# Another hand-kept order of work for a fused attention and feed-forward kernel

## The chip, the core and the metric

The kernel runs on one core of a Trainium2 chip. A core has five engines that matter here, each with its own list of instructions, taken in order: TensorE (PE, matrix products, with a weight load, PEld, ahead of each), VectorE (DVE), ScalarE (ACT), GpSimd (POOL) and SyncE (SP), which here only starts DMA transfers. An engine that must wait for another's result stops, and everything behind that instruction in its list stops too. The metric is the time of one execution in microseconds (us). The kernel before has a median of 922.56 us over three runs (921.46 to 923.68).

## What is computed

The reference is block-sparse attention followed by a feed-forward stage, in fp32:

```python
# q, k, v: (4, 8, 768, 64): 4 batches, 8 heads, 768 positions, 64 per head
scores = scale * np.matmul(q, k.transpose(0, 1, 3, 2))      # scale = 1/8
scores = np.where(mask, scores, -1000000000.0)              # 32-wide blocks: window, edges, 3 drawn per row
attn = np.exp(scores - np.max(scores, axis=-1, keepdims=True))
attn = attn / (np.sum(attn, axis=-1, keepdims=True) + 1e-09)
x = np.matmul(attn, v)                                      # then (3072, 512)
h = x @ w_in                                                # 512 x 2048
out = (h - np.tanh(h)) @ w_out                              # 2048 x 512
```

## The kernel before

**Precision.** Most fp32 products are made from two parts: a high part, rounded to the type that PE multiplies, and a low part, what is left. A product is then three matmuls, high by high, high by low and low by high. Engines therefore spend much time on splits: ACT makes high parts (a copy), DVE or POOL low parts (a subtraction).

**Attention.** The 32 heads are taken in pairs, since two heads fill 128 partitions. The keys and queries of a pair are loaded (`load_qk`), split (`high` L333 on ACT, `low` L339, on DVE for all pairs but the first) and copied by DMA to the places in `slab` that the matmuls read (`dist` L362). V is loaded (`load_v` L327) into a single raw buffer, `rawv`. DVE takes its absolute maximum (`v_max` L417), PE turns that (`v_all` L425), DVE makes a scale (`v_scale`, L429 to L434), ACT the high part (`v_high` L438) and DVE the low part (`v_low` L442). Only then is the raw buffer free for the next pair.

Each head needs the largest score of each row before its exponentials. This is a first pass over the scores: six `smax` units of PE (L455) per head go two by two into the buffer `psm`, and DVE reduces each two in one `maxima` (L461); these two `smax` are called a *smax pair*. PE turns the maxima (`turn_max` L469, again through `psm`), DVE negates them (`neg_max` L473), and a DMA puts them as one more row into the operands of the scores (`put_max` L479).

A head then has three steps of two *score blocks*, 128 keys by 768 queries each: four matmuls (L488, L489) into the buffer `pst`, of which there is one; ACT's exponential (`expo` L492) reads it and writes `pe`. ACT makes the fp16 high part (`p_high` L498, `ph`), POOL the low part (`p_low` L507, `pl`). Two steps later an *accumulate block* on PE (`accum`, L521, L524, L525, 36 short fp16 matmuls) multiplies them with V into `pav`. After a head's last step DVE norms the result (`norm`), and each pair is written out as part of x (`spill` L542).

**Feed-forward.** x is read back, turned by PE in blocks of 128 (`x_turn` L832, four small transposes each) and split (L836, L840). A *unit* is a slice of 128 of the 2048 inner columns for 512 rows of x: twelve matmuls (`h_part` L854) into a bank, then ACT and DVE form h − tanh(h) from a polynomial (L864 to L882), POOL makes its low part (L884), and the second product follows (L889, L890, L891). Units of the first part run among the attention, in halves of six matmuls; they fill PE while exponentials are made. Weights are staged by DMA (`stage_w` L741 and L745) and split; four of them come in through `fetch_w` (L921) and `split_w` (L926 on ACT, L928 on POOL) where attention ends. Everything behind that point is the late part of the plan, and there PE is fed by feed-forward units alone.

**What sets the order.** The kernel builds a list of operations, each with a due time, an engine, an estimated duration, and the buffers it reads and writes (`Plan.add`). The order in each engine's list comes from `ORDER`: a string of characters per engine, where each character says how far down the remaining operations, sorted by due time, the next one lies (`Plan.lanes`):

```python
for c in row:
    if c == MARKS[-1]:
        skip += len(MARKS) - 1
    else:
        lanes[e].append(rest.pop(skip + MARKS.index(c)))
        skip = 0
```

`Plan.order` then walks the five lists with the estimated durations and gives each operation a modelled start. These starts decide only two things: the sequence in which the operations are written down over all engines, which leaves each engine's own order as the strings have it, and the *fillers*. `KeepBusy` puts extra matmuls (L240, `ones` into `pav`) in front of a PE operation where the modelled start leaves a gap, up to 110 us of modelled time; 14 stand at the very start. `in_order` at last chains the instructions of each engine, so that nothing moves them any more.

## Time and profile before

| what | value |
|---|---|
| median of three runs | 922.56 us (921.46 to 923.68) |
| the profiled execution's own time | 921.18 us |
| its span, first to last instruction | 919.4 us |
| mean granted clock of PE | 0.999 |
| PE busy | 895.2 us, 97% of the span |
| DVE, ACT, POOL busy | 76%, 71%, 53% |
| DMA, queue of the loads and stores | 119.58 MB, 45.5% of 16 engines' span |

All instruction times are from that one profiled execution, which was 1.38 us faster than the median. Line numbers in the profile are those of the kernel above. The bracket at the end of a timeline row tells how long the engine stood idle before the instruction, and what released it. In the list of waits, "A <- B: total, times, longest" says that the instruction A of an engine stood for B. A row for PEld is a weight load that had to wait; PE itself may still be working on the matmul before it, so such waits are partly hidden. [...]

### The profile page before, as it was taken

The numbers are of one execution on the slowest core, as the hardware profiler recorded it, in microseconds if no ns is written. First come the engines' busy times: TensorE is split into PE (matmuls) and PEld (weight loads), VectorE is DVE, ScalarE is ACT, GpSimd is POOL, SyncE is SP. The second block draws the span as 40 slices with busy tenths as digits, with TensorE's granted clock in tenths as the row PEclk, the third lists the DMA queues.
The fourth block names the chain that finished last, engine by engine and source line by source line (L and its number), as shares of the span: only waits on it lengthen the run. The fifth ranks groups of instructions, "written<-read, shape, count | busy, mean of one in ns | idle before, by whom it ended". The sixth has DMA issues, their size and how long they took to land.

```text
span 919.4 us, 18275 instructions
## 1 busy us (share of the span) xinstructions
PE 895.2 (97%) x7177; PEld 744.8 (81%) x7177; DVE 701.5 (76%) x1000; ACT 654.0 (71%) x964; POOL 485.4 (53%) x324
## 2 busy tenths in 40 slices
PE   8998999999999999999989999999999999999998
PEld 4777778888887888888878888888888888888886
DVE  6987878889887888886469999985667666765765
ACT  5888888988889798798865666665555555555553
POOL 5677887778777676778842434532212222222131
PEclk9999999999999999999999999999999999999999
DMA  8878588766878758465352333230014202300201
GB/s 228 205 187 240 133 219 225 206 174 178 208 233 193 199 134 278 109 168 178 94 162 92 104 92 94 90 115 1 1 70 155 86 24 92 127 23 1 92 1 46
DMA packets 57677, 120.73 MB, mean 131 GB/s; under 512 B 6170, under 2 KB 26836, under 8 KB 56568
## 3 DMA queue, kind: packets, MB, share of 16 engines
q1 hardware_dynamic: 57592, 119.58, 45.5%
q8 instruction: 56, 0.92, 0.4%
q14 instruction: 29, 0.24, 0.1%
HBM read 55.68 MB, written 26.21 MB: 89 GB/s over the span
## 4 chain that ended last, share of the span: by engine, by line
PE 84%; ACT 6%; DVE 4%; DMA 3%; issue 2%; SPq 1%; POOL 0%; ACTq 0%; DVEq 0%
PE bank L854 27%; PE pf L889 8%; PE pf L891 8%; PE pf L890 8%; PE pst L488 7%; PE pst L489 6%; PE psm L455 5%; PE pav L521 3%; PE pav L524 3%; PE pav L525 3%; ACT pe L492 3%; PE bank L889 1%; DMA raw<-qk 1%; PE bank L890 1%; PE bank L891 1%
## 5 line engine op out<-in xcount | busy, mean ns | idle before, releaser
L507 POOL TENSOR_TENSOR pl<-pe,ph 128x768 f16<-128x768 f32 x192 | 320.4, 1688 | 95.4 <-ACT ph L498 49.8
L884 POOL TENSOR_TENSOR gl<-t,gh 128x512 fp32r<-128x512 f32 x96 | 126.9, 1323 | 298.6 <-ACT gh L882 233.3
L492 ACT ACTIVATE pe<-pst 128x768 f32<-128x768 f32 x192 | 155.2, 808 | 54.1 <-PE pst L489 52.1
L461 DVE TENSOR_REDUCE mc<-psm 128x2 f32<-128x1536 f32 x93 | 163.0, 1753 | 30.5 <-PE psm L455 29.8
L498 ACT ACTIVATE ph<-pe 128x768 f16<-128x768 f32 x192 | 157.9, 840 | 2.7 <-PE pav L525 0.3
L488 PE MATMUL pst<-slab 128*128 128x512 f32 (+1 forms) x384 | 141.6, 369 | 8.7 <-ACT pe L492 7.4
L868 DVE TENSOR_TENSOR t<-t,bank 128x512 f32<-128x512 f32 x96 | 65.7, 684 | 94.3 <-ACT t L866 69.0
L489 PE MATMUL pst<-slab 97*128 97x512 f32 (+1 forms) x384 | 122.4, 340 | 0.0
L521 PE MATMUL pav<-vhl,ph 128*128 128x65 f16 x1152 | 116.4, 194 | 0.1
L524 PE MATMUL pav<-vhl,ph 128*128 128x64 f16 x1152 | 115.8, 195 | 0.0
L525 PE MATMUL pav<-vhl,pl 128*128 128x65 f16 x1152 | 115.3, 192 | 0.0
L521 PEld LDWEIGHTS <-ph 128*128 128x128 f16 x1152 | 105.5, 96 | 7.0 <-issue 4.4
L874 ACT ACTIVATE u<-u,bias 128x512 f32<-128x512 f32 x96 | 69.2, 721 | 58.3 <-DVE bank L876 57.8
L524 PEld LDWEIGHTS <-ph 128*128 128x128 f16 x1152 | 106.6, 97 | 0.4 <-issue 0.2
L525 PEld LDWEIGHTS <-pl 128*128 128x128 f16 x1152 | 106.7, 99 | 0.0
L488 PEld LDWEIGHTS pst<-slab 128*128 128x128 f32 x384 | 72.6, 189 | 32.0 <-ACT pe L492 19.7
L455 PE MATMUL psm<-slab 88*128 88x512 f32 (+1 forms) x378 | 87.9, 350 | 5.9 <-DVE nm L473 1.9
L866 ACT ACTIVATE t<-bank 128x512 f32<-128x512 f32 x96 | 56.7, 591 | 43.5 <-PE bank L854 38.8
L864 ACT ACTIVATE u<-bank 128x512 f32<-128x512 f32 x96 | 57.0, 594 | 43.0 <-PE bank L854 41.8
L882 ACT ACTIVATE gh<-t 128x512 fp32r<-128x512 f32 x96 | 60.3, 628 | 36.3 <-DVE t L880 18.1
L880 DVE COPY_PREDICATED t<-u,bank 128x512 f32<-128x512 int32 x96 | 71.5, 745 | 18.9 <-ACT u L874 13.5
L890 PE MATMUL pf<-wx,gh 128*128 128x512 f32 x216 | 84.1, 389 | 0.0
(135 smaller groups left out, 1918.5 us busy)
## 6 DMA issues: line engine op xcount, KB each, us to landing
slab<-hm SPq DMA_DIRECT2D x124, 192.0 KB
slab<-lo SPq DMA_DIRECT2D x63, 192.0 KB
raw<-qk SPq DMA_DIRECT2D x15, 768.0 KB
stage<-w_in SPq DMA_DIRECT2D x16, 512.0 KB
stage<-w_out SPq DMA_DIRECT2D x16, 512.0 KB
xsav<-xbuf SPq DMA_DIRECT2D x4, 2048.0 KB
rawv<-v SPq DMA_DIRECT2D x16, 384.0 KB
xscr<-xq SPq DMA_DIRECT2D x16, 384.0 KB
```

The costliest lines, as they stand in the source:

```text
L455: nc.tensor.matmul(o[:, b0 + c0 : b0 + c1], lhsT=sB[s][0:88, t * P : (t + 1) * P], rhs=sA[s][0:88, c0:c1], start=True, stop=True)
L461: nc.vector.tensor_reduce(out=mcs[h][:, t - 1 : t + 1], in_=psm.rearrange("p (x s) -> p x s", x=2), op=ALU.max, axis=AX.X)
L488: nc.tensor.matmul(pst[:, q], lhsT=sC[c][:, kc], rhs=sD[c][:, q], start=True, stop=False)
L489: nc.tensor.matmul(pst[:, q], lhsT=sA[a][0:97, kc], rhs=sB[a][0:97, q], start=False, stop=True)
L492: nc.scalar.activation(out=pe[s % 2][:, x * S : (x + 1) * S], in_=pst[:, 0:S], func=AF.Exp, scale=0.125)
L498: nc.scalar.activation(out=phs[s][0][:, c], in_=pe[s % 2][:, c], func=AF.Copy)
L507: eng.tensor_tensor(out=pl[:, c], in0=pe[s % 2][:, c], in1=ph[:, c], op=ALU.subtract)
L521: nc.tensor.matmul(oav[:, t, :], lhsT=ph[:, c], rhs=vv[:, 0:65], start=(kt == 0 and t == 0), stop=False, skip_group_check=True)
L524: nc.tensor.matmul(oav[:, t, 0:64], lhsT=ph[:, c], rhs=vv[:, 65:129], start=False, stop=False, skip_group_check=True)
L525: nc.tensor.matmul(oav[:, t, :], lhsT=pl[:, c], rhs=vv[:, 0:65], start=False, stop=last, skip_group_check=True)
L854: self.nc.tensor.matmul(h, lhsT=w[:, cc], rhs=z[:, c, :], start=(c == 0 and x == 0), stop=(c == NCT - 1 and x == 2))
L890: self.nc.tensor.matmul(o, lhsT=gh[:, c], rhs=wo[1][ft], start=False, stop=False)
```

## The change

All five strings of `ORDER` are replaced, so all five engines run their operations in another order. The operations themselves are the same: same matmuls, same splits, same transfers, except for the fillers. Of the rest of the diff, three things bear on what runs.

- The estimates that `Plan.order` uses change: durations, the time from an engine's end to a reader on another engine (`HOP`, `MORE`), and a result is now ready for a reader on the *same* engine 0.03 us after its latency and not at once. Since the order is given by the strings, these change only the written sequence and the number of fillers.
- High and low parts of the exponentials now lie in one tile with three buffers (`halves`), where there were two tiles with three buffers each. The size is the same, and so are the readers and writers of each part.
- Two small tiles `vf` are added, with a memset each on DVE at the start. Nothing reads them: the options that would (`FULL`, `TWICE`) are empty.

The core of the diff, with one row of a string for all:

```diff
-        "#$%&#&'########(((##&####%%##########%##&#*##(##*&##&*#%##%###&%##$'#%##($#%###&#####&###'###############$#%##"
+        '#$%#%&##%$#####((##&##$##&%#######$$#&%##%##(##&&##&&#%##&%#######$#########################$#$$#$##$#########'
...
+FULL = {}
+TWICE = [s for s in range(1, 27) if s < 0]
...
-    HOP = {"PE": 0.045, "ACT": 0.08, "DVE": 0.03, "POOL": 0.1, "SP": 0.03}
-    LESS = {"PE": 0.0, "ACT": 0.1, "DVE": 0.0, "POOL": 0.0}
-    MORE = {"PE": 0.17, "ACT": 0.1, "DVE": 0.085, "POOL": 0.05}
+    HOP = {"PE": 0.045, "ACT": 0.1, "DVE": 0.05, "POOL": 0.11, "SP": 0.03}
+    LESS = {"PE": 0.0, "ACT": 0.11, "DVE": 0.0, "POOL": 0.01}
+    MORE = {"PE": 0.17, "ACT": 0.11, "DVE": 0.085, "POOL": 0.06}
...
                 if b in wrote:
                     deps[i].add(wrote[b])
+                    reads.add((wrote[b], i))
...
-                    d += 0.09 * (not o[10] and (fp16 or t > free[e] + 0.02))
-                    fp16 = o[10]
+                    d += 0.085 if kind == 2 else 0.09 * (not o[10] and (kind or t > free[e] + 0.02))
+                    kind = int(o[10])
...
                 same = ops[j][2] == e and e != "SP"
-                ready[j] = max(ready[j], free[e] if same else end + self.HOP[ops[j][2]])
+                k = end + 0.03 if (i, j) in reads else free[e]
+                ready[j] = max(ready[j], k if same else end + self.HOP[ops[j][2]])
...
+    vf = [acst.tile([P, 2, 2, 65], F32, name=f"vf{i}") for i in range(NV)]
     for i in range(NV):
         nc.vector.memset(vhl[i][:, :, :, 64:65], 1.0)
+        nc.vector.memset(vf[i][:, :, :, 64:65], 1.0)
...
+    def halves(s):
+        if s not in phs:
+            phs[s] = p2.tile([P, 2, 2, S], F16, tag="ph", name=f"ph{s}", bufs=3)
+        return phs[s]
...
     def p_high(s, x):
-        if s not in phs:
-            phs[s] = [p2.tile([P, W2], F16, tag=n, name=f"{n}{s}", bufs=3) for n in ("ph", "pl")]
         c = slice(x * S, (x + 1) * S)
-        nc.scalar.activation(out=phs[s][0][:, c], in_=pe[s % 2][:, c], func=AF.Copy)
+        nc.scalar.activation(out=halves(s)[:, x, 0], in_=pe[s % 2][:, c], func=AF.Copy)
```

What the new strings move, counted over the plan's operations:

| what | before | after |
|---|---|---|
| between two successive score blocks on PE (191 places): nothing | 2 | 0 |
| only transposes of the maxima or of V's scale | 5 | 4 |
| one `smax` | 2 | 2 |
| two `x_turn` (eight transposes of x) only | 1 | 0 |
| a smax pair, no transposes of x | 34 | 33 |
| a smax pair and `x_turn` | 6 | 9 |
| an accumulate block, half a unit, or more | 141 | 143 |
| between a smax pair and the next use of `psm` (93 places): nothing | 1 | 0 |
| one score block only (all in heads 1 to 9) | 6 | 7 |
| two score blocks | 2 | 0 |
| accumulate blocks followed by work of another kind | 95 | 90 |
| ACT: an exponential directly followed by the copy that reads it | 76 | 52 |
| fillers (of which 14 at the start in both) | 94 | 80 |

On PE, one of the two places where a score block stood directly behind another is the second block of step 13 and the first of step 14 (line L488 and L489 before, L520 and L521 in the changed kernel; `pst` is the buffer of the scores, `psm` that of the maxima). Before:

```order
L488 MATMUL pst<-slab 128x256
L489 MATMUL pst<-slab 128x256
L488 MATMUL pst<-slab 128x512
L489 MATMUL pst<-slab 128x512
L488 MATMUL pst<-slab 128x256
L489 MATMUL pst<-slab 128x256
L455 MATMUL psm<-slab 128x512
```

After:

```order
L520 MATMUL pst<-slab 128x256
L521 MATMUL pst<-slab 128x256
L479 MATMUL psm<-slab 128x512
L479 MATMUL psm<-slab 128x256 x2
L479 MATMUL psm<-slab 128x512
L520 MATMUL pst<-slab 128x512
L521 MATMUL pst<-slab 128x512
L520 MATMUL pst<-slab 128x256
```

The smax pair that stood behind the second of these blocks now stands between the two.

On DVE, at the start of the program, the maxima of head 1 (L461, then L485), a weight's conversion (L751 and L755, then L809), the low part of V for pair 0 (`vhl`; L442, then L448), the low part of keys and queries of pair 1 (`lo1`; L339, then L345) and the negated maxima (`nm`; L473, then L497) stand before as

```order
L461 TENSOR_REDUCE mc1_261<-psm_155 128x2
L751 TENSOR_SCALAR bank1_79<-stage1_82 128x512
L442 SCALAR_TENSOR_TENSOR vhl0_157<-rawv0_242,sb0_320,vhl0_157 128x12x64
L755 SCALAR_TENSOR_TENSOR bank1_79<-stage1_82,bank1_79 128x512
L473 TENSOR_SCALAR nm1_357<-psm_155 6x128
L339 TENSOR_TENSOR lo1_359<-raw1_267,hm1_316 128x1536
```

and after as

```order
L485 TENSOR_REDUCE mc1_265<-psm_155 128x2
L448 SCALAR_TENSOR_TENSOR vhl0_157<-rawv0_188,sb0_283,vhl0_157 128x12x64
L485 TENSOR_REDUCE mc1_265<-psm_155 128x2
L345 TENSOR_TENSOR lo1_327<-raw1_269,hm1_312 128x1536
L497 TENSOR_SCALAR nm1_377<-psm_155 6x128
L809 TENSOR_SCALAR bank0_78<-stage0_81 128x512
```

V's low part moved ahead of the last maximum, the conversions behind the negated maxima, and the low part of pair 1 between the last maximum and the negated ones. On SP, the loads of a part of `w_in` and of `w_out` stood ahead of the load of pair 1's keys and queries; now `w_out` stands ahead of it and `w_in` behind.

On SP, the load of V for pair 11 (`rawv11`; L327, then L333) stands before among the copies to `slab` (L362) of pairs 10 and 11, behind a put of maxima (L479):

```order
L479 DMA slab_80<-nm21_4519 1x6x128
L362 DMA slab_80<-hm10_3851 64x768
L362 DMA slab_80<-hm11_4407 64x768 x2
L327 DMA rawv11_4593<-v 128x768
L542 DMA xscr2_62<-xq8_4001 768x1x128
```

and after directly behind the load of keys and queries of pair 12 (L323), ahead of those entries:

```order
L368 DMA slab_80<-lo10_4166 64x768
L323 DMA raw12_4457<-qk 128x1536
L333 DMA rawv11_4551<-v 128x768
L886 DMA stage0_81<-xscr1_61 128x512
L368 DMA slab_80<-hm11_4148 64x768
L503 DMA slab_80<-nm21_4438 1x6x128
```

On DVE the reader of that load moved with it. With a pair's V loaded only after the low part of the V before, it matters how much DVE work lies between the two: between `v_low` of one pair and `v_max` of the next stood at most one `maxima` for the pairs 9, 12 and 15 before, and for 4, 5, 6, 9 and 11 after. For pair 11 the operations between went from eleven to four.

Where attention ends, six matmuls of a unit (half of `h_part`) move behind the last score block on PE, between two of the last feed-forward products. POOL's four low parts of weights (L928) stood in the order second product of weight 4, first product of 4, first of 5, second of 5; now first of 5, second of 4, first of 4, second of 5. The first that PE reads there is the first product's weight 4.

## Prediction on record

> **What bounds the kernel now.** I read the page first, then four long stretches, then the list of waits, then single places of the timelines.

> ```profile
> span 919.4 us, 18275 instructions
> ...
> PE 895.2 (97%) x7177; PEld 744.8 (81%) x7177; DVE 701.5 (76%) x1000; ACT 654.0 (71%) x964; POOL 485.4 (53%) x324
> ...
> PEclk9999999999999999999999999999999999999999
> ```

> TensorE (PE) is busy for 97% of the span, at full granted clock. A new order takes no matmul away (fillers aside), so it can win only what PE spends waiting. The stretches (duration, then busy time and instructions of PE, PEld, DVE, ACT, POOL, then clock, DMA share, GB/s) show where that lies:

> ```profile
> 0.00:30.00 30.00, 25.73 (x142) 15.07 (x142) 21.71 (x38) 19.30 (x25) 15.87 (x17) 1.00 0.82 225
> 30.00:140.00 110.00, 101.88 (x1307) 84.67 (x1306) 92.66 (x116) 93.93 (x118) 86.68 (x52) 1.00 0.77 198
> 140.00:480.00 340.00, 332.14 (x3814) 286.26 (x3811) 266.66 (x361) 290.13 (x401) 254.18 (x157) 1.00 0.66 182
> 480.00:915.00 435.00, 434.79 (x1923) 358.66 (x1921) 319.77 (x487) 250.67 (x422) 128.69 (x100) 1.00 0.20 68
> ```

> From 480 to 915 us PE idles 0.21 of 435 us: there a new order wins nothing and can only lose. Before 480 us it idles 4.27 + 8.12 + 7.86 = 20.3 us, and fillers hide more. That is the whole field. The waits (total us, times, longest) name the first cause:

> ```profile
> ACT pe L492 <- PE pst L489: 52.1, 101, 2.6
> ...
> PEld pst L488 <- ACT pe L492: 19.7, 40, 1.2
> ...
> DVE am L417 <- DMA rawv<-v: 6.3, 5, 2.6
> ```

> Scores and exponential share one buffer, `pst`. PE's weight loads wait 19.7 us for ACT's exponential to empty it, and ACT waits 52.1 us for scores: a loop of two engines, each late for the other.

> **Term 1, the loop through `pst`.** What a score block costs when too little stands behind it:

> ```profile
> 76.61 0.50 PE L488 MATMUL pst<-slab 128*128 128x512 f32 x1
> ...
> 78.54 0.50 PE L488 MATMUL pst<-slab 128*128 128x512 f32 x1 [0.96 <-ACT pe L492]
> ...
> 79.36 0.86 PE L455 MATMUL psm<-slab 88*128 88x512 f32 x4
> 80.48 0.50 PE L488 MATMUL pst<-slab 128*128 128x512 f32 x1 [0.26 <-ACT pe L492]
> ```

> From block to block it is 1.93 us with nothing between (from 76.61) and 1.94 us with a smax pair between (from 78.54). The block alone keeps PE 0.82 us (78.54 to 79.36), so 1.12 us want covering. A pair covers 0.7 of them and leaves 0.4; an accumulate block or half a unit covers all. The table of the change then gives: two places with nothing go, 2 x 1.12 = 2.24; one of five with only the maximum's or V's transposes goes, which I put at 0.9, between the 0.4 left by a pair and 1.12; the place with eight transposes of x goes, 0.4 as for a pair; one pair place goes, 0.4. That is 3.9 us. Counted like this the old order would wait 2 x 1.12 + 5 x 0.9 + 2 x 0.75 (one smax) + 0.4 + 34 x 0.4 = 22.2 us, where the row says 19.7, so I scale by 0.89: **-3.5 us**. Bounds: -2.2 (the empty places alone) and -3.9.

> **Term 2, the maxima and the start.** The same for `psm`, which a smax pair fills and DVE's maximum (L461) empties:

> ```profile
> 21.25 0.97 PE L455 MATMUL psm<-slab 88*128 88x512 f32 x4 [0.28 <-DVE mc L461]
> ...
> 24.09 0.27 PE L469 MATMUL psm<-ident,mc 128*6 128x128 f32 x1 [0.34 <-DVE mc L461]
> ...
> 49.44 0.86 PE L455 MATMUL psm<-slab 88*128 88x512 f32 x4
> ...
> 52.15 0.97 PE L455 MATMUL psm<-slab 88*128 88x512 f32 x4 [0.61 <-DVE mc L461]
> ```

> From a pair to the next use of `psm` it is 2.7 to 2.8 us, 0.7 of it the pair itself. With one score block between, 0.9 us stay open (2.71 - 0.70 - 1.12); with nothing, 2.1. The table has "nothing" 1 to 0 and "one score block" 6 to 7, in heads 1 to 9: -2.1 + 0.9 = -1.2 us. The place with nothing is the start, where the next step hangs on DVE:

> ```profile
> 22.28 1.75 DVE L461 TENSOR_REDUCE mc<-psm 128x2 f32<-128x1536 f32 x1
> 23.95 0.69 DVE L751 TENSOR_SCALAR bank<-stage 128x512 int32<-128x512 int32 x1
> 24.96 1.02 DVE L442 SCALAR_TENSOR_TENSOR vhl<-rawv,sb,vhl 128x768 f16<-128x768 f32 x1 [0.33 <-ACT vhl L438]
> 25.89 0.69 DVE L755 SCALAR_TENSOR_TENSOR bank<-stage,bank 128x512 int32<-128x512 int32 x1
> 26.49 0.27 DVE L473 TENSOR_SCALAR nm<-psm 6x128 fp32r<-6x128 f32 x1
> 26.69 1.74 DVE L339 TENSOR_TENSOR lo<-raw,hm 128x1536 fp32r<-128x1536 f32 x1
> ```

> From the last maximum to the negated maximum, for which the fourth step's scores wait, are 4.21 us. In the new order one `low` (L339) stands between: 1.67 + 1.74 = 3.4 us, 0.8 sooner. But `low` hangs on the second pair's load, and nothing shows that to land earlier by more than the one weight load that no longer precedes it. Both gains lie on one chain, so I do not add them in full: **-1.5 us**; bounds -2.5 and, should the load hold `low`, +1.0.

> **Term 3, changes of kind.** The first score matmul behind an accumulate block takes 0.32 us to the next start, another 0.23:

> ```profile
> 448.61 0.48 PE L488 MATMUL pst<-slab 128*128 128x512 f32 x1
> 448.93 0.40 PE L489 MATMUL pst<-slab 97*128 97x512 f32 x1
> ...
> 450.76 0.39 PE L488 MATMUL pst<-slab 128*128 128x512 f32 x1
> 450.99 0.40 PE L489 MATMUL pst<-slab 97*128 97x512 f32 x1
> ```

> 95 such changes become 90: 5 x 0.09 = **-0.45 us**; bounds -0.45 and 0.

> **Term 4, the passage to the second stage.** PE waits there for POOL's low part of a weight (L928):

> ```profile
> 466.16 0.61 PE L854 MATMUL bank<-xbuf,slab 128*128 128x512 f32 x2
> 468.31 2.56 PE L854 MATMUL bank<-xbuf,slab 128*128 128x512 f32 x10 [1.54 <-POOL slab L928]
> ...
> 465.75 5.01 POOL L928 TENSOR_TENSOR slab<-slab 128x512 fp32r<-128x512 f32 x4
> ```

> The four take 1.25 us each; the one PE needs first was second and is now third, +1.25 us. Against it, half a unit (six matmuls, 1.4 us) now stands behind the last scores and lets PE arrive later, but POOL's work on that unit also starts later. I take **+0.9 us**; bounds -0.5 and +2.0.

> **What I cost at nothing.** The search's own point, that a result reaches the next instruction of its engine late, is in ACT's rows:

> ```profile
> 449.66 0.81 ACT L492 ACTIVATE pe<-pst 128x768 f32<-128x768 f32 x1 [1.26 <-PE pst L489]
> 450.37 1.57 ACT L498 ACTIVATE ph<-pe 128x768 f16<-128x768 f32 x2
> ...
> 453.81 0.81 ACT L492 ACTIVATE pe<-pst 128x768 f32<-128x768 f32 x1 [1.18 <-PE pst L489]
> 454.66 0.85 ACT L498 ACTIVATE ph<-pe 128x768 f16<-128x768 f32 x1
> ```

> The copy at 450.37 reads an older exponential and starts 0.71 us after the one ahead; that at 454.66 reads the one just made and starts after 0.85. 24 fewer such pairs are 24 x 0.14 = 3.4 us of ACT time. The 52.1 us in which ACT waits for scores cover it, so 0; without that cover, -3.4. [...]

> The load of V for pair 11 moves ahead of two entries that wait, but its reader on DVE moves ahead too (rival 2): 0; bounds -1.7 and +1.7, the price of one such wait below.

> **Sum.** -3.5 - 1.5 - 0.45 + 0.9 = -4.55 us. On the profiled execution (921.18 us, 1.78 around its span) that is 916.6; its median of three, 922.56, is 1.38 above it, so 922.56 - 4.55 = **918.0 us**. All bounds at their good ends: -3.9 - 2.5 - 0.45 - 0.5 - 3.4 - 1.7 = -12.4, so 910.1; at their bad ends: -2.2 + 1.0 + 0 + 2.0 + 1.7 = +2.5, so 925.1.

> **Rivals.** (1) *ACT is the slower half of the loop.* Then its 3.4 us come through, and with term 1 unscaled (-0.4) the time is 914.2, by the bounds down to 910. For it: ACT's 94 of 110 us from 30 to 140 us. Against it: ACT waits for PE more than twice as long as PE for ACT.

> (2) *DVE is held by the loads of V; slower.* V has one raw buffer, so the load of pair p starts only after DVE's low part (L442) of pair p-1, and DVE stops at the next pair's absolute maximum (L417) until it lands. What one such stop did:

> ```profile
> 296.20 0.40 PE L891 MATMUL bank<-wo,gl 128*128 128x512 f32 x1
> 298.08 0.96 PE L455 MATMUL psm<-slab 88*128 88x512 f32 x4 [1.48 <-DVE nm L473]
> ```

> DVE stood up to 2.6 us, and PE 1.88 - 0.23 = 1.65 us. In the new order five pairs (4, 5, 6, 9, 11) have at most one pair maximum between the two, against three (9, 12, 15) before, and the load for pair 11 now stands right behind one of 768 KB. If all five stop PE like that, where one did before, it is 4 x 1.65 = 6.6 us more: 922.56 - 4.55 + 6.6 = 924.6. It decides from three further stops on (4.95 us). Against it: two of the three short places before cost PE nothing that shows.

> (3) *Waits move, none goes.* POOL, DVE and DMA are 77 to 84% busy from 30 to 140 us, so PE may find the next late partner at each place: 922.6.

> A fourth: 14 fewer fillers, and the clock drops for a while. The first 14 fillers of the run show what that costs:

> ```profile
> 1.45 5.78 PE L240 MATMUL pav<-ones 128*128 128x512 f16 x14 [1.45 <-DVE ones L267]
> ...
> 22.06 1.69 PE L240 MATMUL pav<-ones 128*128 128x512 f16 x7
> ```

> They take 413 ns each, later ones 241, so one slow stretch costs 14 x 0.172 = 2.4 us and gives 920.4. PE's longest wait under 480 us was about 2 us and the clock stayed at 1.00, so I give it 0.03, within the forecast's case. [...]

> **Chances.** Forecast (about 918) 0.45; rival 1 0.18; rival 3 0.17; rival 2 0.20. About 0.2%, 1.85 us, is what a measurement of this kernel can tell from no change. So faster 0.63, the same 0.17, slower 0.20. The likeliest case alone spans 914 to 920.5. The range for 8 in 10 goes from 909, just beyond the good ends, to 926, which holds rival 2 with one stop more than it counts: **909 to 926**.

> **What would show it.** Term 1: PEld's wait on L492's successor falls from 19.7 to about 16 us. Terms 1 and 2: PE's idle time before 480 us falls from 20.3 to 16 or less, more of it before 140 us than after. Term 4: the wait on POOL's weight parts grows to 2 or 3 us. Rival 1: ACT's wait for scores falls by less than PE's wait for ACT. Rival 2: DVE's wait for `rawv` grows beyond 10 us. Idle PE between 480 us and the end would be something that I have priced at zero, and would prove me wrong first.

## The result, and the profile after

The changed kernel takes 934.39 us (median of four runs, 928.87 to 939.17), the kernel before 922.01 beside it. The ratio is 1.014 (95% interval 1.0108 to 1.0173): 12 us slower, where 4.6 us faster was forecast, and outside the range. The profiled execution took 934.74 us. Medians and ratios here leave out two slow executions of over 3 ms, one of e8 and one of e9.

From the page of the changed kernel, the span, the busy times, the slices of the granted clock, and the shares of the chain that ended last:

```profile
span 932.7 us, 18255 instructions
...
PE 901.2 (97%) x7163; PEld 747.4 (80%) x7163; DVE 701.0 (75%) x1002; ACT 652.9 (70%) x964; POOL 486.1 (52%) x324
...
PEclk9999999999999999999989999999999999999999
...
PE 71%; DVE 13%; DMA 6%; ACT 5%; issue 3%; SPq 1%; POOL 0%; ACTq 0%; DVEq 0%; POOLq 0%
```

One slice of the clock shows an 8. On the chain, PE has 71% where it had 84%, and DVE and DMA 19% where they had 7. Before:

```profile
PE 84%; ACT 6%; DVE 4%; DMA 3%; issue 2%; SPq 1%; POOL 0%; ACTq 0%; DVEq 0%
```

The stretches, with the same columns as in the prediction:

```profile
0.00:30.00 30.00, 25.57 (x150) 15.99 (x151) 22.19 (x38) 17.09 (x22) 17.90 (x17) 1.00 0.81 219
30.00:140.00 110.00, 101.66 (x1317) 85.57 (x1316) 92.66 (x118) 94.47 (x121) 83.28 (x50) 0.98 0.76 196
140.00:480.00 340.00, 327.00 (x3751) 282.40 (x3750) 263.89 (x355) 285.63 (x394) 256.27 (x158) 0.99 0.64 181
480.00:915.00 435.00, 432.99 (x1892) 352.17 (x1891) 313.33 (x479) 250.73 (x420) 124.82 (x97) 0.99 0.21 69
```

Idle PE was to fall before 480 us. It rose from 20.3 to 25.8 us (4.43 + 8.34 + 13.0), and from 480 to 915 us, where it had been 0.21, it is 2.0. Three of the four rows show a clock below 1.00. The waits of the changed kernel:

```profile
ACT pe L527 <- PE pst L521: 55.1, 88, 3.1
...
PEld pst L520 <- ACT pe L527: 12.6, 29, 0.9
...
PEld bank L912 <- DVE t L938: 9.9, 24, 1.0
...
PEld psm L479 <- DVE mc L485: 8.1, 12, 1.7
...
DVE am L423 <- DMA rawv<-v: 7.3, 5, 2.5
```

The wait on the exponential fell by 7.1 us, twice the forecast. Two others grew: on the maxima (8.1), and, in the late part, on a unit's selection (L938, L880 before) that must leave the PSUM bank before PE can fill it again (9.9). The same two rows of the kernel before:

```profile
PEld psm L455 <- DVE mc L461: 3.1, 8, 0.8
...
PEld bank L854 <- DVE t L880: 2.5, 5, 0.8
```

Two marks that every trace has, the start of the last score block and the first turn of x behind attention (`T`), split the span. "Half" counts stretches of half clock ahead of the last few us; the last column is the start of step 12's scores.

| kernel | last score block | T | span | between the two | T to the end | half | step 12 |
|---|---|---|---|---|---|---|---|
| before | 454.9 | 474.1 | 919.4 | 19.2 | 445.3 | 0 | 70.1 |
| changed | 455.5 | 479.6 | 932.7 | 24.1 | 453.1 | 4 | 68.7 |
| changed, a second trace (e16 below) | 452.8 | 476.9 | 927.7 | 24.1 | 450.8 | 0 | 69.2 |

So of 13.3 us, attention has some 0.5, the passage 4.9 and the part behind it 7.9; how much of this hangs on the clock is taken up below. Attention scatters from one execution to the next: its last score block starts between 452.8 and 455.8 us in five traces with the new order up to there (changed, e2, e4, e15, e16; in e5, with half a unit more ahead of it, at 461.0), and between 453.3 and 458.7 in eight with the old one (before, e1, e3, e8, e12, e13, e14, e17). The other two parts repeat to a few tenths.

### The profile page after: what moved, and what is told of

Same layout as the page of the kernel before. It is cut to its first block, busy times and chain, and to the rows that moved or that the text cites. A ratio compares the mean times of both kernels' runs of the same rounds, so it can differ in the third digit from the quotient of the medians.

```text
span 932.7 us, 18255 instructions
## 1 busy us (share of the span) xinstructions
PE 901.2 (97%) x7163; PEld 747.4 (80%) x7163; DVE 701.0 (75%) x1002; ACT 652.9 (70%) x964; POOL 486.1 (52%) x324
## 4 chain that ended last, share of the span: by engine, by line
PE 71%; DVE 13%; DMA 6%; ACT 5%; issue 3%; SPq 1%; POOL 0%; ACTq 0%; DVEq 0%; POOLq 0%
PE bank L912 22%; PE pf L947 6%; PE pf L948 6%; PE pf L949 6%; PE pst L520 6%; PE pst L521 5%; PE psm L479 4%; PE pav L563 3%; PE pav L566 3%; PE pav L567 3%; DVE mc L485 2%; ACT pe L527 2%; DMA rawv<-v 2%; PE bank L947 1%; PE bank L948 1%
## 5 line engine op out<-in xcount | busy, mean ns | idle before, releaser
L540 POOL TENSOR_TENSOR ph<-pe,ph 128x768 f16<-128x768 f32 x192 | 324.0, 1707 | 104.3 <-issue 46.5
L942 POOL TENSOR_TENSOR gl<-t,gh 128x512 fp32r<-128x512 f32 x96 | 124.1, 1294 | 313.2 <-ACT gh L940 273.1
L527 ACT ACTIVATE pe<-pst 128x768 f32<-128x768 f32 x192 | 155.1, 808 | 59.4 <-PE pst L521 55.1
L485 DVE TENSOR_REDUCE mc<-psm 128x2 f32<-128x1536 f32 x93 | 163.2, 1755 | 33.4 <-PE psm L479 32.2
L520 PE MATMUL pst<-slab 128*128 128x512 f32 (+1 forms) x384 | 141.9, 369 | 5.8 <-ACT pe L527 4.0
L926 DVE TENSOR_TENSOR t<-t,bank 128x512 f32<-128x512 f32 x96 | 65.6, 684 | 89.8 <-ACT t L924 51.2
L521 PE MATMUL pst<-slab 97*128 97x512 f32 (+1 forms) x384 | 123.2, 342 | 0.0
L563 PE MATMUL pav<-vhl,ph 128*128 128x65 f16 x1152 | 117.4, 195 | 0.1
L567 PE MATMUL pav<-vhl,ph 128*128 128x65 f16 x1152 | 116.2, 193 | 0.0
L932 ACT ACTIVATE u<-u,bias 128x512 f32<-128x512 f32 x96 | 69.2, 721 | 62.9 <-DVE bank L934 62.4
L563 PEld LDWEIGHTS <-ph 128*128 128x128 f16 x1152 | 106.0, 97 | 6.4 <-issue 3.1
L566 PEld LDWEIGHTS <-ph 128*128 128x128 f16 x1152 | 107.3, 98 | 0.3 <-issue 0.3
L567 PEld LDWEIGHTS <-ph 128*128 128x128 f16 x1152 | 107.4, 100 | 0.0
L479 PE MATMUL psm<-slab 88*128 88x512 f32 (+1 forms) x378 | 89.5, 351 | 8.4 <-DVE mc L485 5.1
L520 PEld LDWEIGHTS pst<-slab 128*128 128x128 f32 x384 | 73.0, 190 | 25.9 <-ACT pe L527 12.6
L948 PE MATMUL pf<-wx,gh 128*128 128x512 f32 x216 | 84.1, 389 | 0.0
L947 PE MATMUL pf<-wx,gh 128*128 128x512 f32 x216 | 84.1, 389 | 0.0
L949 PE MATMUL pf<-wx,gl 128*128 128x512 f32 x216 | 84.1, 389 | 0.0
L521 PEld LDWEIGHTS pst<-slab 97*128 97x128 f32 x384 | 73.6, 192 | 11.0
```

Source lines behind the costliest of these rows:

```text
L485: nc.vector.tensor_reduce(out=mcs[h][:, t - 1 : t + 1], in_=psm.rearrange("p (x s) -> p x s", x=2), op=ALU.max, axis=AX.X)
L520: nc.tensor.matmul(o, lhsT=sC[c][:, kc], rhs=sD[c][:, c0:c1], start=True, stop=False)
L521: nc.tensor.matmul(o, lhsT=sA[a][0:97, kc], rhs=sB[a][0:97, c0:c1], start=False, stop=True)
L527: nc.scalar.activation(out=o[:, c0:c1], in_=area[:, 0 : c1 - c0], func=AF.Exp, scale=0.125)
L540: eng.tensor_tensor(out=pl, in0=pe[s % 2][:, c], in1=ph, op=ALU.subtract)
L563: nc.tensor.matmul(oav[:, t, :], lhsT=ph[:, c], rhs=vv[:, 0:65], start=(kt == 0 and t == 0), stop=False, skip_group_check=True)
```

## Experiments

In all diffs that name operations, `S` is a score block (step.half), `A` an accumulate block, `m` a smax unit, `H` a first product of a feed-forward unit (slice of rows.unit.half), `O` a second one. The kernels are made from the changed one by other strings; where another line changes, the diff has it.

### e1, e2, e3: which part of the change

```diff
e1:  all lists:  old order        (estimates, merged tile, memsets: new)
e2:  attention:  new order        late part: old order
e3:  attention:  old order        late part: new order
```

> The changed kernel with the five strings of the kernel before: estimates, the merged tile and the two memsets are new, the order is old. Because the new estimates see larger gaps in the old order, it has 113 fillers (before 94, changed 80). If the order alone costs the time (my theory): 922 us, within 2 of the kernel before, clock 1.00 throughout. If the merged tile of high and low parts or the memsets cost it: near 934 us.

> The changed kernel, but everything behind the end of attention in the order of before; the attention part, with the last three accumulate blocks behind the feed-forward halves, is the new one. Theory: three separate losses, attention with two stretches of half clock (about 0.5 us in sum against before), the passage (19.2 us from the last score block to the first turn of x before, 24.15 after, and some 3 us of half clock behind it) and the new order of the late part (some 4.5 us of short waits for DVE's selection). Only the last goes: 929 to 930 us. Rival, the late waits are only the consequence of the late passage: 934 us. Second rival, the late order is the whole loss: 922 us.

> The opposite: attention in the order of before, the part behind it in the new one. Theory of three separate losses: 922 + 4.5 = 926 to 927 us. Rival, late waits are a consequence of the late passage: 922 us. Second rival, the late order is the whole loss: 932 us or more.

| kernel | median us | ratio to before (interval) | last score block to T | T to the end | half |
|---|---|---|---|---|---|
| e1 | 923.90 | 1.0012 (0.9984 to 1.0040) | 19.2 | 445.2 | 1 |
| e2 | 928.24 | 1.0065 (1.0038 to 1.0091) | 26.4 | 446.6 | 3 |
| e3 | 928.06 | 1.0068 (1.0044 to 1.0092) | 19.2 | 451.1 | 1 |

The old order in the new code is as fast as the kernel before: the table is the cause, and neither the merged tile nor more fillers (113 here). The passage's loss goes with the new attention order (7.2 us in e2, where PE waits 5.6 us for the load of x), the late part's 5 to 6 us with the new late order, each without the other. e3 came 1 to 2 us slower than the theory, e2 1 faster; both rivals fall.

### e4, e5: the passage

In the changed kernel's timelines of PE, SP, ACT and POOL around the passage:

```profile
479.60 1.09 PE L890 MATMUL pf<-ident,wx 128*128 128x128 f32 x4 [3.37 <-DMA wx<-xscr]
```

```profile
473.14 0.56 SPq L584 DMA_DIRECT2D xscr<-xq  x1
476.66 1.30 SPq L886 DMA_DIRECT2D wx<-xscr  x3
```

```profile
459.46 0.60 ACT L924 ACTIVATE t<-bank 128x512 f32<-128x512 f32 x1 [2.14 <-PE bank L912]
459.96 0.84 ACT L531 ACTIVATE ph<-pe 128x768 f16<-128x768 f32 x1
```

and the same two entries of SP before:

```profile
464.63 0.56 SPq L542 DMA_DIRECT2D xscr<-xq  x1
...
468.06 1.75 SPq L828 DMA_DIRECT2D wx<-xscr  x4
```

PE waits 3.4 us for a load of x. In both kernels that load is issued 3.4 to 3.5 us behind the spill of the last heads (`xscr<-xq`), and the spill is 8.5 us later than before, since the last three accumulate blocks and the norm behind them are: the first of the three starts 11.7 us behind the start of the last score block, before 2.1. Half a unit ahead of them had moved behind the last score block; ACT's first work on it (459.46) stands 2.14 us for it, with the copies of the last exponentials behind it.

e4 puts the accumulates back, e5 the half unit too:

```diff
 PE  S95.0 O3.0.0 S95.1 O3.0.1
-    H3.2.1 O3.0.2 O3.0.3 H3.3.0 H3.3.1 A93 A94 A95
+    A93 H3.2.1 O3.0.2 A94 O3.0.3 A95 H3.3.0 H3.3.1        e4
 DVE ... o_out selection
-    unit H3.3, norm
+    norm, unit H3.3                                       e4 and e5
+PE  S95.0 O3.0.0 H3.2.1 S95.1 O3.0.1 A93 O3.0.2 A94 ...   e5
```

> The changed kernel, with one place put back: the last three accumulate blocks stand between the feed-forward products as before, and the last norm on DVE ahead of the last unit's operations. Theory: the wait of 3.5 us for the loads of x and the half clock behind it go, 934 - 4.9 - 3 = 926 to 927 us. Rival, the late waits follow from the passage: 922 us. Rival, the passage is not the cause of the wait for x (the loads wait for something else): 934 us.

> The run before it (last accumulate blocks put back), and also the half unit that had moved behind the last score block put back in front of it. In the run before, 24.4 us still passed from the last score block to the first turn of x (19.2 in the kernel before). Theory: ACT's first operation on that unit stands ahead of the last copies of exponentials and of the weight splits, so ACT stood 2 to 3 us for the half unit and everything behind it, POOL's splits too, was late. With the half unit back: 21 to 22 us there, and 927 to 928 us in all (2.5 less than 930.9). Rival, only the order of POOL's four splits holds the first late unit (the one it needs is third, 1.25 us each): still 24 us, and 931.

e4 took 930.91 us (1.0097, 1.0070 to 1.0124), where 926 to 927 was expected. It is 3.5 us below the changed kernel's median, but in its trace the passage still takes 24.4 us. The load of x is in time there, and PE stands ahead of it, at the first late unit, for POOL's weight part:

```profile
470.05 0.61 PE L912 MATMUL bank<-xbuf,slab 128*128 128x512 f32 x2
473.42 6.89 PE L912 MATMUL bank<-xbuf,slab 128*128 128x512 f32 x22 [2.75 <-POOL slab L986]
480.15 0.60 PE L890 MATMUL pf<-ident,wx 128*128 128x128 f32 x4
```

In e4 an accumulate block stands ahead of the half unit, and ACT waits 3.33 us for the half unit, where it waited 2.14. POOL's splits of the weights then start 13.8 us behind the last score block (in the changed kernel 11.5, before 10.8). With the half unit back as well (e5), the splits start at 10.9 us, and the passage takes 19.8 us in the trace, against 24.4, although POOL's splits keep their new order. So two things are late in turn: in the changed kernel the accumulate blocks hold the load of x, and with these put back the half unit, through ACT, holds the splits. The rival, POOL's order alone, falls; what that order costs shows in e5, where PE's weight load waits 3.3 us for POOL, against 2.0 in e6 below, which has the old end. No run put the half unit back alone, so its share in the changed kernel is not measured. The time did not follow: 930.61 us (1.0091, 1.0065 to 1.0116), where 927 to 928 was expected. In e5's profiled execution the last score block starts at 461.0 us, 5 us later than in e4's, with two stretches of half clock in attention to e4's one; the mean clock over the runs was 0.995, in e4 0.996. Why attention was so late in that execution is open.

### e6, e7: the new attention order alone, and V

> New attention order up to the last steps; the end of attention (last score blocks, last accumulates, splits) and all behind it in the old order. Theory, the passage and the late order are the whole loss and the new attention order is even: 19 us from the last score block to the first turn of x, 2 us of waits behind it, 920 to 922 us. Rival, the new attention order itself loses some 2 to 4 us to stops of DVE for its loads: 923 to 925 us.

```diff
e7:
-        rawv[pr] = p2.tile([P, 2 * T, D], F32, tag="rawv", name=f"rawv{pr}", bufs=1)
+        rawv[pr] = p2.tile([P, 2 * T, D], F32, tag="rawv", name=f"rawv{pr}", bufs=2)
-    vf = [acst.tile([P, 2, 2, 65], F32, name=f"vf{i}") for i in range(NV)]
-        nc.vector.memset(vf[i][:, :, :, 64:65], 1.0)
```

> The run before it with two raw buffers for V, for which the two unused small tiles and their memsets are left out. A load of V then waits no longer for the low part of the V before. Theory (loads of V stop DVE, and DVE's maxima then stop PE): DVE's wait for V falls from some 6 to 7 us to under 2, and 2 to 4 us go: 917 to 919 us. Rival, the load is late because of its place in SP's queue and not for the buffer, or DVE stops at its next load instead: the same as the run before it, 920 to 924 us.

e6 took 922.96 us (1.0018, 1.0005 to 1.0030), on the border between its theory and the rival: its passage takes 19.2 us and the rest 445.2, and the new attention order up to the last steps wins nothing; by the interval it is 0.5 to 2.8 us slower. e7 took 926.31 (1.0046, 1.0023 to 1.0069), slower than e6, where 917 to 919 was expected. The waits of e6 and of e7 from 30 to 455 us:

```profile
DVE am L423 <- DMA rawv<-v: 6.1, 4, 3.0
...
PEld pst L520 <- ACT pe L527: 12.3, 30, 0.9
PEld psm L479 <- DVE mc L485: 6.9, 10, 2.0
```

```profile
DVE am L421 <- DMA rawv<-v: 3.6, 4, 1.7
...
PE bank L888 <- DMA stage<-xscr: 1.4, 1, 1.4
...
PEld pst L518 <- ACT pe L525: 14.1, 33, 0.9
PEld psm L477 <- DVE mc L483: 5.2, 10, 1.6
```

The second buffer takes 2.5 us from DVE's wait for V and 1.7 from PE's for the maxima; the wait on the exponential takes 1.8 back, and other loads come late (L888). The waits move, as the third rival of the prediction had it. For the 3.6 us that DVE still waits for V, the load's place in SP's queue is a likely reason, which no run shows. DVE's stops in the changed kernel are not for V alone:

```profile
223.78 0.70 DVE L809 TENSOR_SCALAR bank<-stage 128x512 int32<-128x512 int32 x1 [1.86 <-DMA stage<-w_in]
...
298.55 0.95 DVE L423 TENSOR_REDUCE am<-rawv 128x1 f32<-128x768 f32 x1 [2.09 <-DMA rawv<-v]
```

### e10, e11: the start and the middle

```diff
e10: up to step 24's scores: new order    from there: old order
e11: up to step 24's scores: old order    from there to the end of attention: new order    then: old order
```

> The new order up to step 24's scores (some 118 us), the old one from there to the end. Theory: the new start is really better, by the 2.5 us less of lost PE time there (30.1 against 32.6), and the new middle loses that again to stops of DVE for loads: 919 to 920 us. Rival, the gain at the start is lost again at the seam or is only scatter: 922 us.

> The opposite: the old order up to step 24's scores, the new one from there to the end of attention, and the old end. Theory: only the loss of the new middle remains, 2 to 4 us: 924 to 926 us. Rival, the middle is even: 922 us.

e10 took 924.97 us (1.0049, 1.0031 to 1.0068), e11 926.13 (1.0067, 1.0051 to 1.0083). e11 is at the upper end of its theory, e10 5 us above its own. But both are slower than the whole new attention order (e6), so the cut itself costs: e10 has two stretches of half clock right behind it, at 118.9 us. They can't price the two halves. What the traces do show is the start: step 12's scores begin at 66.6 to 69.9 us in ten traces with the new order there (the changed kernel, e2, e4 to e7, e9, e10, e15, e16), and at 70.1 to 71.9 in nine with the old one (the kernel before, e1, e3, e8, e11 to e14, e17). The new start is better by some 2.5 us on average (68.3 against 70.8), and since e6 wins nothing in all, the middle gives it back.

### e9, e15, e16: the clock

```profile
27.70:31.10 3.40, 2.03 (x12) 1.45 (x10) 2.33 (x3) 1.09 (x2) 1.70 (x2) 1.00 0.97 279
31.10:34.50 3.40, 3.40 (x41) 3.11 (x41) 2.77 (x3) 2.48 (x4) 1.64 (x1) 0.50 0.93 268
225.70:229.10 3.40, 1.91 (x28) 1.46 (x27) 3.40 (x5) 2.37 (x3) 2.89 (x3) 1.00 0.41 104
229.10:232.50 3.40, 3.40 (x29) 3.01 (x26) 2.92 (x3) 0.78 (x2) 1.27 (x1) 0.50 0.25 77
474.80:478.25 3.45, 1.43 (x7) 0.85 (x5) 2.68 (x4) 1.32 (x3) 0.00 (x0) 1.00 0.41 107
478.25:485.10 6.85, 5.50 (x17) 4.53 (x18) 2.59 (x4) 1.69 (x3) 0.00 (x0) 0.50 0.64 217
```

The busy column reads higher than the work, since matmuls overlap in the record: the one at 450.76 us of the kernel before lasts 0.39 us, and the next starts 0.23 us behind it. Counted by what each matmul takes back to back, PE had work for some 48, 48 and 36% of the three stretches ahead of half clock. I took all 19 traces apart along their grids, some 5,000 stretches at full clock, and counted this share for each. Below 40%, 22 of 24 were followed by half clock; from 40 to 50%, 12 of 37; from 50 to 65%, 1 of 122; above, none of 4,865. These are counts from the records of this case, and e9 and e15 were to test what they suggest by filling PE's waits.

```diff
e9 (on e6):  fillers ahead of step 3's scores (32), of smax units of heads 10, 13, 17 (20 each) and of head 22's turn (24)
e15 (on the changed kernel):
+            if o[4].__name__ == "turn" and o[5][:3] == (4, 0, 0):
+                for _ in range(15):
+                    nc.tensor.matmul(ffn.banks[3], lhsT=ones[:, 0:P], rhs=ones, start=True, stop=True)
```

> The new attention with the old end (measured 922.96, mean granted clock 0.997 over its executions), with 20 to 32 filler matmuls in front of the five places where PE waited longest (step 3, heads 10, 13, 17 and 22), none longer than the wait it stands in. In all traces so far the half-clock stretches last 3.413 us, lie on a fixed grid of 3.413 us, and follow a stretch of that grid in which PE was busy for 0 to 49 % of the time. Theory: a wait of 1.5 to 2 us costs a half-clock stretch whenever it falls into one stretch of the grid; with the waits filled the mean clock is 0.999 or more in nearly all executions, and the time 1 to 2 us less, 921 to 922. Rival, the clock falls for another reason: clock 0.997 and 923 us as before.

> The changed kernel with 15 filler matmuls (512 columns, some 3.3 us) in front of the first turn of x, where PE waits 3.5 us for a load; nothing else moves. In the changed kernel two half-clock stretches (6.83 us) follow that wait, and the turns and second products in them take some 2.5 to 3 us longer. Theory: a stretch of the 3.413 us grid in which PE is busy for less than about half halves the clock in the next; with the wait filled both stretches go: mean clock 0.003 to 0.004 higher than in the unedited changed kernel beside it, and 2 to 3 us faster. Rival: the clock falls there for another reason, or the loads behind the wait set the time anyway: the same time as the changed kernel beside it.

> The changed kernel as it is, for comparison on the same chip in the same rounds: 932 to 936 us, mean clock 0.992 to 0.995, half-clock stretches behind the passage in its profile.

e9 took 928.65 us (1.0071, 1.0043 to 1.0098), 6 us more than without the fillers, at the same clock. Its time says nothing against or for what the counts suggest, since the fillers made waits of their own: two of the five groups wait for DVE's norm (0.27 and 2.42 us), which reads the same bank. At head 13:

```profile
161.66 1.23 PE L246 MATMUL pav<-ones 128*128 128x122 f16 x20 [2.42 <-DVE xq L580]
```

In e6 PE stood 1.17 us there. At 27 and 128 us, where the fillers waited for nothing and for 0.27 us, no half clock followed, where e6 had one behind each.

e15 took 931.20 us (1.0092, 1.0071 to 1.0114), e16, the changed kernel beside it, 933.86 (1.0118, 1.0096 to 1.0141). The direction and the size (2.7 us) are as forecast, but the intervals overlap. Its trace shows what the fillers did: T stays at 24.0 us behind the last score block, and the clock behind it is full: T to the end takes 450.6 us, where the changed kernel's first trace has 453.1.

```profile
476.20 3.41 PE L299 MATMUL pf<-ones 128*128 128x512 f16 x15
479.58 0.63 PE L893 MATMUL pf<-ident,wx 128*128 128x128 f32 x4
```

A trace with the grid in another place came by chance. e16's profiled execution had the same wait of 3.40 us, and no half clock at all: the wait fell across two stretches of its grid, which by the count above were busy for some 47 and 45%, in the band where 12 of 37 stretches were followed by half clock.

```profile
core 0: 927.7 us, clock 1.000
```

```profile
471.78:475.19 3.41, 1.76 (x8) 1.13 (x6) 2.68 (x4) 1.63 (x3) 0.00 (x0) 1.00 0.47 120
475.19:478.60 3.41, 1.66 (x12) 1.51 (x13) 0.36 (x1) 0.99 (x2) 0.00 (x0) 1.00 0.81 283
```

It took 929.86 us, the first trace of the same program, with four stretches of half clock, 934.74. Of the 4.9 us between them, 2.4 lie behind T, where two of the stretches are, and that part repeats to a few tenths otherwise. The rest lies in attention, with the other two, and that it is their cost is not shown: e3's five executions spread from 925.42 to 930.00 us at mean clocks of 0.998 to 1.000. With no half clock, the changed kernel is still 8.3 us behind the kernel before (927.7 to 919.4): -2.1 in attention (within its scatter), +4.9 in the passage, +5.5 behind it.

### e8, e12, e13, e14, e17: the late part

e8, e12, e13 and e14 start from e3 and edit one engine's list in the late part, or two.

```diff
e8   DVE: each unit's five operations (L926 to L938) together, 74 of 80 units without other work between (17 in the new order, 27 in the old)
e12  ACT: a unit's two reads of the bank (L922, L924) and its second square (L930) together
e13  PE:  units moved behind second products until 6.8 us of matmuls lie between a unit and the next but one
e14  e8 and e12 together
```

> Attention in the old order, the late part in the new order (measured 928.1), and on DVE alone, in the late part, each unit's five operations put together: 74 of 80 units have nothing between their first and last operation there (17 in the new order, 27 in the old). Theory: in the new order other work stands between the five, which makes the chain from a unit's matmuls to the end of its selection 0.8 us longer, and PE's next but one unit waits for that: waits of PE there fall from 7.9 us to 3 or less, 923 to 924 us. Rival, it is PE's own order, whose units stand less evenly: 928 us.

> Attention in the old order, the late part in the new one (measured 928.1, waits of PE in the late part 7.9 us, with the old late order 2.0), and on ACT alone, in the late part, each unit's first read of the bank and its square stand directly behind the other read. In the new order these two start 0.4 and 0.8 us later behind the unit's matmuls than in the old one, and the selection 0.7 us later. Theory ACT: this lateness is what PE waits for; the waits fall to 3 us or less, 923 to 924 us. Theory PE: the units stand less evenly in PE's own order, and no other engine can mend that: still 6 to 8 us of waits, 927 to 929. Theory DVE (conversions inside the chains): also unchanged.

> The same base, and on PE alone, in the late part, units are moved behind one or more second products where fewer than 6.8 us of matmuls lie between a unit and the next but one, which takes its bank: 13 such places in the new order become 2 (old order: 6). Theory PE: waits fall from 7.9 to 3 us or less, 923 to 924 us. Theories ACT and DVE: the chains stay long, so at most 1 to 2 us go: 926 to 928.

> The same base with ACT's steps as in the first of these runs, and DVE's five operations of a unit together as in the run that put only those together and took 954 us with 34 us of waits. If that one failed because ACT's order still interleaved the units, so that DVE stood at the first operation whose input was late: waits below 10 us and 923 to 930 us. If whole chains on DVE are bad in themselves, since they leave DVE waiting for ACT inside each unit: again more than 25 us of waits, 945 to 955.

| kernel | median us | ratio to before (interval) |
|---|---|---|
| e8 | 953.97 | 1.0341 (1.0314 to 1.0368) |
| e12 | 957.59 | 1.0388 (1.0355 to 1.0420) |
| e13 | 938.73 | 1.0188 (1.0164 to 1.0211) |
| e14 | 985.25 | 1.0682 (1.0643 to 1.0721) |

All four are far slower than e3 (928.06), and every theory here missed, e14's second alternative in size too. The row on the bank, from 486 to 915 us, of e3 and of e12:

```profile
PEld bank L912 <- DVE t L938: 10.1, 24, 1.1
```

```profile
PEld bank L912 <- DVE t L938: 35.8, 37, 2.3
```

The order of one engine is fitted to those of the others: a square moved ahead on ACT pushes back what other units need there, and in e8 PE waits most for DVE's reads of the second products (L1009, 9.9 us) and less for the bank (7.7). Such edits show that coupling, and nothing on which list is at fault. So the last run left all lists as e3 has them, and took away the thing that PE waits for:

```diff
-                self.unit_ops(plan, d if x else d + 0.2, n, ft, u % 2, ("bank", u % 2), xi, u % 2, ...
+                self.unit_ops(plan, d if x else d + 0.2, n, ft, u % 3 if u > 11 else u % 2,
+                              ("xt",) if u > 11 and u % 3 == 2 else ("bank", u % 3 if u > 11 else u % 2), xi, u % 2, ...
         self.banks, self.xt, self.cv = banks[:4], banks[4], banks[5]
+        self.hb = [*self.hb, self.xt]
```

> Attention in the old order and the late part in the new one (measured 928.1), and from the twelfth unit of the late part on the units take three PSUM banks in turn instead of two (the third is free by then); no order is changed. In the new late order PE's weight loads wait 10.1 us for a unit's selection to leave its bank (1.7 us with the old late order). Theory: the new late order plans the units so close behind the selection that frees their bank that small delays reach PE; with a third bank these waits fall below 3 us, PE's waits in the late part from 7.9 to some 3 us, and the time to 923 to 925. Rival: the selections are late because ACT and DVE as a whole are behind, and then PE waits for the second products' operands instead: 927 to 928.

e17 took 923.87 us (1.0022, 1.0005 to 1.0039), 4.2 less than e3, and T to the end is 445.1 us, as in the kernel before, where e3 has 451.1. The same row, of e17 and, with the old late order, of e1:

```profile
PEld bank L912 <- DVE t L938: 1.8, 4, 1.2
```

```profile
PEld bank L912 <- DVE t L938: 1.7, 4, 0.6
```

So the late order's whole loss runs over the bank. No run gave the third bank to the old late order, so what it would win there is not measured. Where that lateness comes from can be read from the lists and the trace: averaged over the 80 late units, the selection starts 6.9 us behind the unit's last matmul in e3 and in e17, and 6.1 in e1: the third bank takes away what the lateness costs, and not the lateness. ACT's second square (L930) starts 3.2 us behind in e3 against 2.4 in e1, and 2.3 foreign operations stand among a unit's five on DVE where 1.5 did. The new order puts other work between a writer and its reader more often, and each unit's chain gets longer by that work. Which of the two engines' lists sets it is not settled.

## Why the prediction was wrong, point by point

**What bounds the kernel.** Right: PE's waits are the field. The sentence that from 480 us on a new order "wins nothing and can only lose" was right too, and the step that failed comes straight behind it: that loss entered the sum with 0 and the bounds not at all. It measured 5.5 us without half clock (445.3 to 450.8): with it alone the sum would have been 923.5 us in place of 918.0, outside the 914 to 920.5 of the likeliest case. The cost was the bank, which the lengthened chains free later (e17). The lists of that part differ as much as the others, and I had counted nothing there.

**Term 1**, -3.5 us. Right in mechanism, too small: the row fell from 19.7 to 12.6.

**Term 2**, -1.5 us. The start is indeed ahead at step 12, by 2.5 us on average over the traces and by 0.9 and 1.4 us in the changed kernel's own two. The waits on the maxima grew all the same, from 3.1 to 8.1 us in PEld's row. DVE itself stopped longer for loads (below), and in e7, where it stopped less for V, the row fell from 6.9 to 5.2. Terms 1 and 2 together gave 2.1 us in the attention of the execution without half clock, where 5.0 was forecast; part of that 2.1 is the half unit, 1.4 us, that was merely moved behind the last score block. The rest is less than the scatter of attention, so no gain of these two terms in time is shown.

**Term 3**, -0.45 us: too small to be told from the scatter of attention in any run.

**Term 4**, +0.9 us, bounds to +2.0. This is the term that was wrong by most of its size: the passage takes 4.9 us more, or 3.5 without the 1.4 us of moved work. The prediction looked only for what the first late unit waits for, POOL's parts. Its +1.25 us for their order was right where it could show (3.3 against 2.0 us in e5 and e6), but in the changed kernel PE does not stop for POOL there at all. The end of attention has another end, the last accumulate, norm, spill and load of x, which the order had pushed 8.5 us back. The three accumulate blocks moved in the lists, but the section on the change does not name that move, and the prediction did not follow it to the load. The half unit, booked as cover, held ACT 2.14 us.

**Costed at nothing.** That a reader next to its writer costs more holds in the rows (0.85 against 0.71 us on ACT in the kernel before, 0.727 and 0.800 against 0.604 on DVE in e3). ACT's 24 fewer such pairs brought no time, as forecast: its wait for scores stayed (52.1, then 55.1). DVE stopped for V 7.3 us, not the 10 that rival 2 named, but for V and other loads together its waits grew: from 30 to 470 us they are 3.7 us before and 11.9 after. Rival 2 had the mechanism, with too narrow a name, and e7 shows that its cure moves the wait on.

**The fourth case**, half clock, had a chance of 0.03 and one stretch at 2.4 us. I had taken the longest wait in one piece for the measure, which was 1.5 us below 480 us and not about 2. In the records the half clock goes with PE's share of the stretch of the grid ahead of it (below 40%, 22 of 24 were followed by it, from 40 to 50%, 12 of 37), and stretches with waits of 1.92 us in all (e6), or of 0.96 and 0.27 (e1), had it behind them. The price was my estimate from the first fillers, for whose time the trace has no clock on record (it begins at 6.72 us), and it was too high: the two stretches behind the passage cost 2.4 us together, 1.2 each. The number of fillers does not decide it: e1 has 113 fillers and a stretch of half clock in its trace, the changed kernel 80 and, in its second trace, none.

**The range**, 909 to 926, summed the bounds of the places I had counted. A table that rewrites every list has places one has not counted, and the range had nothing for them. Nor does it quite hold rival 2 with one stop more, which is 924.6 + 1.65 = 926.25 us.

## What to carry to other kernels

A new order has to be followed to the end of each list, above all where the profile says that nothing is lost: there it can only lose, and a full engine shows no cover for what becomes late. At a passage between two stages, follow every chain that crosses it (here a unit's reads, the weight parts, and spill and load) from the operation that moved, not from the wait that stands there now. An order that wins a little engine time by putting other work between dependents pays for it where buffers turn over: look for the pair of buffers that the longer chain holds, and see whether a third is free.

## What the runs showed of the hardware

The half clock was not expected in this form. In these traces it comes in stretches of 3.413 or 6.827 us on a grid that is fixed within an execution (in the changed kernel at 31.111, 229.084 and 478.257 us, 58 and 73 steps of 3.413 us apart) and lay elsewhere in another execution of the same program (a step at 478.26 us in the first trace, at 478.60 in the second). Of the full-clock stretches of such grids in which PE had work for less than 40% of the time, 22 of 24 were followed by half clock, of those from 40 to 50% 12 of 37, of those above 1 of 4,987. Waits of 1.92 us in one stretch (e6), or of 0.96 and 0.27 us (e1), had half clock behind them. In the first trace of the changed kernel two stretches at half clock behind the passage cost 2.4 us, which the trace of the same program without half clock does not have (453.13 against 450.76 us from T to the end).

On DVE, a reader directly behind its writer started 0.727 us after a tensor-tensor operation (L928 to L934, 56 cases) and 0.800 us after a scalar-tensor-tensor one (L934 to L936, 46 cases), where an independent operation started after 0.604 (L926 to L928, 45 cases; 0.601 to 0.605 also behind L928 and L934 where another unit's L938 follows): medians of e3's trace from 480 us on. That is 0.12 and 0.20 us more for the reader; the new estimates have 0.115 (0.085 and 0.03) for both.
